# Attention with q/k norm, then a gated MLP: whole gated units before attention, rstd behind the exponential, and earlier transfer issues

## Chip, cores, metric

One core of one Trainium2 chip. The metric is device time of one execution in microseconds (us), the median of several; spans and stages come from one profiled execution per kernel. The same kernel varies by about 1% from execution to execution, so small differences are judged by ratios with a 95% interval. A run is called slow when it is over 1.5% above the fastest run of the same kernel; the others are fast, and ratios use fast runs alone.

## The reference, cut to what matters

```python
# q, k, v: (8 batches, 12 heads, 448, 64) f32
q_n, k_n = rmsnorm(q, g_q), rmsnorm(k, g_k)
attn = softmax(q_n @ k_n.T / 8)
x = (attn @ v) as (8, 448, 768)
h = relu(x @ w_in)                       # 768 x 1024, halves u and v
v_n = (v - mean) / sqrt(var + 1e-6)
gated = u * (w_spatial @ v_n + b_spatial)
out = gated @ w_out                      # 512 x 768
```

## The kernel before

Heads are taken in 24 groups of four (three groups a batch). A group has seven passes of scores; after 20 early passes (steps 0 to 9) the kernel goes in steps of two passes, 10 to 83. Each step does scores on TensorE, one exponential on ScalarE, and beside it either an attention (three weighings of 16 matmuls) or a slice of the gated MLP of an earlier batch. GpSimd squares and scales q and k and issues the v and weight transfers; VectorE reduces and empties PSUM.

```python
work = deque()                       # gated work, one matmul per entry
def fill(us_of_pe):
    debt[0] = min(debt[0] + us_of_pe, us_of_pe)
    while work and (debt[0] > 0 or work[0][0] == 0):
        cost, fn = work.popleft(); debt[0] -= cost; fn()
# a unit (v: 6 matmuls, u: 6, spatial: 4, out: 4) takes one of four PSUM
# buffers at its first matmul and is emptied after its last

def early(p):                        # ... cut
    if p == 3:
        rstd(1); scaled(1, 0, eng=dve); scaled(1, 1, eng=dve); after((1, 1))
        load_v(0, range(5)); load_w_in(1)
    elif p == 8:
        rstd(2); scaled(2, 0, eng=dve); scaled(2, 1); squares(3, 0); squares(3, 1)
    # ...
for s in range(S0, NST):             # S0 = 10, NST = 84
    scores(pss[:, 0:2], 2 * s); scores(pss[:, 2:4], 2 * s + 1)
    prep(s, True)                    # rstd of the groups due in this step
    expo(pss, 2 * s, 2)
    prep(s, False)                   # reductions, scaling, squares, transposes, loads
    # ...
    if s == 11: load_v(1, range(5))
    if s == 13: load_w_sp()
    if s == 21: load_w_out()
    # ...
    if s in busy: attend(...)        # three weighings: three PSUM buffers
    else: fill(rate)
```

`rstd` is a logarithm and an exponential on ScalarE over the reduced squares.

## Time and profile before

| | before |
|---|---|
| median | 312.6 us (310.65 to 316.51 in the first four) |
| span of the profiled run | 312.4 us |
| exponential of step 10, 14, 25, 83 starts at | 45.00, 60.43, 100.64, 281.61 us |
| TensorE idle, step 25 to 83 | 180.97 - 172.17 = 8.80 us |
| half-clock windows after the start | at 31.9, 59.2, 79.7, 96.7 us, 3.4 us each |

The start of the exponential of a step is my clock through the program. "Early" below is up to step 25, "steady" is step 25 to 83, and then come some 30.7 us of the last batch. In a wait line, "A <- B: total, times, longest" is idle time of A's engine ended by B. Line numbers in a profile are kept from the kernel before, so `L379` is weighing, `L350` scores, `L357` the exponential, `L385` the first instruction of the reciprocal of the sums (which frees the first weighing's PSUM buffer), `L330` the k scale.

This is the view of TensorE's waits in the steady stretch of the kernel before:

```profile
PE pss L350 <- ACT et L357: 2.5, 4, 1.0
PE ps L379 <- ACT rc L385: 1.7, 3, 0.6
PE pss L350 <- DVE kT L330: 1.6, 2, 0.9
PE ps L530 <- DVE osb L435: 1.4, 3, 0.5
```

Six kinds of wait (the four largest are shown; 8.5 us in all), none above 1 us at a time.

### The profile page before, as it was taken

How to read it: one execution, taken by the hardware profiler on the slowest of the kernel's cores; microseconds unless marked ns; L12 is line 12 of the kernel's file. 1: busy time of each engine (PE TensorE's matmuls, PEld its weight loads, DVE VectorE, ACT ScalarE, POOL GpSimd, SP SyncE). 2: the span in 40 equal slices, each digit the busy share in tenths (PEclk: the TensorE clock that was granted, in tenths of full speed). 3: DMA queues.
4: the chain of work that ended last, by engine and by line, in shares of the span. 5: the costliest groups of instructions: out<-in, count | busy, mean ns of one | idle time of the engine just before them, and what ended most of it. 6: DMA issues, size and time to landing. Idle time of an engine off the chain costs nothing.

```text
span 312.4 us, 6419 instructions
## 1 busy us (share of the span) xinstructions
PE 275.7 (88%) x2541; PEld 128.2 (41%) x2541; DVE 208.4 (67%) x360; ACT 205.5 (66%) x260; POOL 201.9 (65%) x185
## 2 busy tenths in 40 slices
PE   7585769599797999998999899989999999999994
PEld 7342324244243444334434443444343444444552
DVE  3863465596675674795896777768867955754652
ACT  2676487489393797758677776866877866765421
POOL 3245679939996499749983999569966960400300
PEclk9789799799797999999999999999999999999999
DMA  7899997966999979999979999999851595121135
GB/s 168 200 248 190 228 213 112 139 156 132 177 138 235 208 125 245 220 223 131 233 100 224 212 135 257 245 162 178 147 96 27 58 201 101 27 101 52 25 153 177
DMA packets 97504, 49.98 MB, mean 160 GB/s; under 512 B 67009, under 2 KB 93826, under 8 KB 97474
## 3 DMA queue, kind: packets, MB, share of 16 engines
q1 hardware_dynamic: 74562, 40.71, 61.5%
q0 software_dynamic: 21552, 8.27, 23.8%
q10 hardware_dynamic: 1360, 0.59, 0.8%
q8 instruction: 20, 0.33, 0.4%
q14 instruction: 10, 0.08, 0.1%
HBM read 38.55 MB, written 11.01 MB: 159 GB/s over the span
## 4 chain that ended last, share of the span: by engine, by line
PE 46%; POOL 14%; DVE 14%; DMA 9%; ACT 8%; issue 6%; SPq 2%; POOLq 0%; DVEq 0%
PE ps L530 9%; PE ps L379 9%; PE ps L458 9%; PE ps L498 7%; PE pss L350 6%; POOL sqt L233 6%; ACT et L357 5%; DMA qb<-in_q_dram 3%; POOL n L260 3%; POOL vn L480 3%; DMA vt<-in_v_dram 3%; DVE ms L241 3%; PE ps L488 2%; DVE s L466 2%; DMA w_out<-in_moe_w_out_dram 2%
## 5 line engine op out<-in xcount | busy, mean ns | idle before, releaser
L357 ACT ACTIVATE et<-pss 128x1792 bf16<-128x1792 f32 x74 | 122.8, 1659 | 48.0 <-PE pss L350 46.3
L241 DVE TENSOR_REDUCE ms<-sqt 128x14 f32<-128x896 f32 x46 | 49.3, 1076 | 13.9 <-POOL sqt L233 13.9
L393 DVE TENSOR_TENSOR xt<-ps,rc 128x448 bf16<-128x448 f32 x48 | 27.9, 619 | 40.9 <-ACT rc L386 40.8
L530 PE MATMUL ps<-w_out,gt 128*128 128x384 bf16 (+1 forms) x256 | 48.9, 333 | 4.1 <-DMA w_out<-in_moe_w_out_dram 2.3
L458 PE MATMUL ps<-w_in_v,xt 128*128 128x512 bf16 (+1 forms) x192 | 48.1, 389 | 0.0
L379 PE MATMUL ps<-et,vt 128*32 128x448 bf16 x768 | 43.1, 359 | 5.5 <-DMA vt<-in_v_dram 3.8
L350 PE MATMUL pss<-qT,kT 64*128 64x448 bf16 x254 | 37.6, 359 | 11.4 <-ACT et L357 5.0
L260 POOL TENSOR_TENSOR n<-kb,rs 128x896 bf16<-128x896 f32 x22 | 38.6, 1753 | 5.4 <-issue 4.5
L488 PE MATMUL ps<-xt,w_in_u 128*128 128x448 bf16 x192 | 40.6, 354 | 1.3 <-ACT vs L427 0.8
L476 POOL TENSOR_SCALAR nm<-mv 128x4 f32<-128x4 f32 x8 | 1.8, 223 | 57.9 <-DVE mv L467 50.1
L233 POOL TENSOR_TENSOR sqt<-qb 128x896 f32<-128x896 f32 x21 | 36.1, 1719 | 0.1
L233 POOL TENSOR_TENSOR sqt<-kb 128x896 f32<-128x896 f32 x21 | 35.3, 1681 | 0.6 <-DMA kb<-in_k_dram 0.6
L435 DVE COPY osb<-ps 128x384 f32<-128x384 f32 (+1 forms) x50 | 27.2, 556 | 12.0 <-PE ps L530 10.5
L260 POOL TENSOR_TENSOR n<-qb,rs 128x896 bf16<-128x896 f32 x18 | 30.5, 1694 | 5.9 <-ACT rs L250 5.7
L530 PEld LDWEIGHTS <-gt 128*128 128x128 bf16 (+1 forms) x256 | 24.7, 102 | 22.1 <-issue 8.6
L379 PEld LDWEIGHTS <-vt 128*32 128x32 bf16 x768 | 21.0, 98 | 22.9 <-DMA vt<-in_v_dram 4.5
L116 POOL DMA_DIRECT2D vt<-in_v_dram x40 | 29.3, 739 | 0.0
L498 PE MATMUL ps<-w_spT,vn 128*128 128x448 bf16 (+1 forms) x128 | 28.7, 369 | 0.3 <-DVE w_spT L209 0.3
L480 POOL TENSOR_SCALAR vn<-vs,nm,rv 128x512 bf16<-128x512 bf16 (+1 forms) x32 | 24.0, 762 | 7.5 <-ACT rv L475 5.1
L350 PEld LDWEIGHTS <-kT 64*128 64x128 bf16 x276 | 10.3, 94 | 41.2 <-issue 28.3
L458 PEld LDWEIGHTS <-xt 128*128 128x128 bf16 (+1 forms) x192 | 18.0, 102 | 21.8 <-issue 7.3
L488 PEld LDWEIGHTS <-w_in_u 128*128 128x128 bf16 x192 | 17.3, 98 | 22.5 <-issue 8.9
(84 smaller groups left out, 325.5 us busy)
## 6 DMA issues: line engine op xcount, KB each, us to landing
out_dram<-osb SPq DMA_DIRECT2D x24, 384.0 KB, 4.4
qb<-in_q_dram SPq DMA_DIRECT2D x7, 576.0 KB, 5.5
qb<-in_q_dram SPq DMA_DIRECT2D x14, 288.0 KB, 6.6
kb<-in_k_dram SPq DMA_DIRECT2D x7, 576.0 KB, 7.6
kb<-in_k_dram SPq DMA_DIRECT2D x14, 288.0 KB, 7.4
vt<-in_v_dram POOLq DMA_DIRECT2D x8, 288.0 KB, 5.4
vt<-in_v_dram POOLq DMA_DIRECT2D x16, 144.0 KB, 4.4
qb<-in_q_dram SPq DMA_DIRECT2D x22, 96.0 KB, 5.3
```

The lines of the kernel that those rows point to most:

```text
L116: pool.dma_start(out=t[r, hs, D * c:D * (c + n)], in_=x)
L233: pool.tensor_tensor(out=t, in0=x, in1=x, op=ALU.mult)
L241: dve.tensor_reduce(out=sqs[gk][:, key[1], :], in_=sqt.pop(key).rearrange("p h c d -> p (h c) d"), axis=AX.X, op=ALU.add)
L260: (eng or pool).tensor_tensor(out=t.rearrange("p c h d -> p h c d"), in0=raw[key], in1=rst[gk][:, key[1], :].rearrange("p (h c) -> p h c", ...
L350: pe.matmul(out=ps[:, h, 0:S], lhsT=kT[r, c0:c0 + 128], rhs=qT[r, :], start=True, stop=True, tile_position=(64 * h, 0))
L357: act.activation(out=ets[s][:, 2 * a:2 * a + 2 * m, :], in_=ps[:, 0:2 * m, 0:S], func=AF.Exp, bias=0.0, scale=1.0)
L379: pe.matmul(out=ps[32 * l:32 * l + 32, 0:S], lhsT=w, rhs=et_of(G, 3 if r == 3 else r + 4 * y, h), start=(r == 0), stop=(r == 3), tile_posi ...
L458: pe.matmul(out=ps[0:m, :], lhsT=xts[b][:, j, t0:t0 + m], rhs=w_in_v[:, j, :], start=(j == 0), stop=(j == 5), tile_position=(0, 0))
L480: pool.tensor_scalar(out=vn_t[b % 2][0:m, c, :], in0=vs[b][c][0:m, :], scalar1=nms[b][0:m, c:c + 1], scalar2=rvs[b][0:m, c:c + 1], op0=ALU ...
L488: pe.matmul(out=ps[:, 0:S], lhsT=w_in_u[:, j, 128 * f:128 * f + 128], rhs=xts[b][:, j, :], start=(j == 0), stop=(j == 5))
L498: pe.matmul(out=ps[:, 0:S], lhsT=vn_t[b % 2][0:kp, c, 128 * f:128 * f + 128], rhs=w_spT[0:kp, c, :], start=(c == 0), stop=(c == NT - 1))
L530: pe.matmul(out=ps[o:o + m, 0:384], lhsT=gts[b][f][:, t0:t0 + m], rhs=w_out[:, f, r], start=(f == 0), stop=(f == 3), tile_position=(0, o))
```

## The change

Intent: leave no unit half done over an attention, keep the rstd chain from holding up exponentials, and use GpSimd's idle time for transfers needed soon.

```diff
-            for part in (0, 2, 3):
+            for part in (0, 2):          # part 3 (first Y rows) now from GpSimd
                 load_part(0, i, part, g)
...
-    def fill(us_of_pe):
+    def fill(us_of_pe, whole):
         debt[0] = min(debt[0] + us_of_pe, us_of_pe)
-        while work and (debt[0] > 0 or work[0][0] == 0):
+        while work and (debt[0] > 0 or work[0][0] == 0 or (whole and not work[0][2])):
...
-            fill(rate)
+            fill(rate, s + 1 in busy)
...
     squares(0, 1, 0)
+    for g in (1, 2):
+        for i in (1, 0):
+            load_part(0, i, 3, g, pool)
...
     after((0, 1, 1))
-    squares(2, 1)
+    load_v(0, range(5))
...                                        # early(3)
-            load_v(0, range(5))
+            squares(2, 1)
...                                        # early(8)
             squares(3, 1)
+            load_v(1, range(5))
...
-            if (what == "rstd") != early_act:
+            if (what == "rstd" and G < 5) != early_act:
...
-        if s == 11:
-            load_v(1, range(5))
-        if s == 21:
+        if s == 19:
             load_w_out()
```

`part 3` is one piece of the "Y rows", the rows of q and k of batch 0's heads 6 to 11; `w_in_v` and `w_in_u` below are the two halves of `w_in`. `work[0][2]` is true at the first matmul of a unit. In the list of a batch's gated work the second u unit also moves ahead of the layer norm's rstd and application.

More of the change, by code (lines that the diff above doesn't have):

```diff
@@ L445, in one @@
                 done(cell[0])
-        return [(each, lambda i=i: one(i)) for i in range(n)]
+        return [(each, lambda i=i: one(i), i == 0) for i in range(n)]
     def tokens(c):
@@ L548, in tails, with also @@
         ot = unit_o(b - 1, 3, 0) + unit_o(b - 1, 3, 1)
-        seq = [(0.216 * i, 0.12, fn) for i, (_, fn) in enumerate(vt)]
-        seq += [(0.163 * i - 0.01, 0.08, fn) for i, (_, fn) in enumerate(ot)]
-        return [(cost, fn) for _, cost, fn in sorted(seq, key=lambda x: x[0])]
+        seq = [(0.216 * i, 0.12, u[1]) for i, u in enumerate(vt)]
+        seq += [(0.163 * i - 0.01, 0.08, u[1]) for i, u in enumerate(ot)]
+        return [(cost, fn, i == 0) for i, (_, cost, fn) in enumerate(sorted(seq, key=lambda x: x[0]))]
     work = deque()
+    def also(fn):
+        work.append((0, fn, True))
     def gated(b):
-        work.extend(unit_v(b, 0) + unit_v(b, 1) + [(0, lambda: stats(b, 0))])
-        work.extend(unit_v(b, 2) + [(0, lambda: stats(b, 1))])
-        work.extend(tails(b) + [(0, lambda: stats(b, 2)), (0, lambda: stats(b, 3))])
-        work.extend(unit_u(b, 0) + [(0, lambda: ln_rstd(b))])
-        work.extend([(0, lambda c=c: ln_apply(b, c)) for c in range(NT)])
-        for f in (1, 2, 3):
-            work.extend(unit_u(b, f))
+        work.extend(unit_v(b, 0) + unit_v(b, 1))
+        also(lambda: stats(b, 0))
+        work.extend(unit_v(b, 2))
+        also(lambda: stats(b, 1))
+        work.extend(tails(b))
+        also(lambda: stats(b, 2))
+        also(lambda: stats(b, 3))
+        work.extend(unit_u(b, 0) + unit_u(b, 1))
+        also(lambda: ln_rstd(b))
+        for c in range(NT):
+            also(lambda c=c: ln_apply(b, c))
+        work.extend(unit_u(b, 2) + unit_u(b, 3))
         if b == 0:
-            work.append((0, bias_row))
-            work.extend((0.5, lambda sc=sc: w_sp_unit(sc)) for sc in range(NT))
+            also(bias_row)
+            work.extend((0.5, lambda sc=sc: w_sp_unit(sc), True) for sc in range(NT))
         else:
@@ L572 @@
     debt = [0.0]
-    def fill(us_of_pe):
+    def fill(us_of_pe, whole):
         debt[0] = min(debt[0] + us_of_pe, us_of_pe)
-        while work and (debt[0] > 0 or work[0][0] == 0):
-            cost, fn = work.popleft()
+        while work and (debt[0] > 0 or work[0][0] == 0 or (whole and not work[0][2])):
+            cost, fn, _ = work.popleft()
             debt[0] -= cost
```

## The prediction

> **What bounds the kernel now.** I read the page's slices first, then the waits of TensorE, then the timelines. From the page, busy tenths of TensorE and its granted clock in 40 slices of 7.8 us:
> ```profile
> PE   7585769599797999998999899989999999999994
> ...
> PEclk9789799799797999999999999999999999999999
> ```
> From slice 13 (about 100 us) TensorE is full and its clock whole; before that there are holes, and each low clock digit sits at or just after one. The busy time of the engines in stretches (busy us with counts for PE, PEld, DVE, ACT, POOL; clock, DMA share, GB/s) puts sizes on it:
> ```profile
> 20.00:40.00 20.00, 13.01 (x148) 6.36 (x150) 10.09 (x13) 12.13 (x19) 10.96 (x13) 0.91 1.28 214
> 40.00:60.00 20.00, 14.18 (x157) 6.17 (x153) 11.82 (x16) 13.04 (x19) 18.58 (x18) 0.98 1.07 157
> ...
> 80.00:100.00 20.00, 16.37 (x116) 6.85 (x115) 11.91 (x21) 10.47 (x13) 19.11 (x15) 0.84 1.17 183
> ```
> TensorE idles about 5.8 us a 20 us stretch up to 60 us, and 3.6 us in 80 to 100. In 100 to 280 the same view sums to 171.2 us busy of 180: only 8.8 us are idle there. After 282 us comes the last batch, nearly all TensorE. So the gain must come mostly from the first 100 us.
>
> The waits of the whole run (us in total, times, longest) name the holes:
> ```profile
> ACT et L357 <- PE ps L379: 7.1, 1, 7.1
> ...
> POOL w_in_v L189 <- DMA vt<-in_v_dram: 3.8, 1, 3.8
> PE ps L379 <- DMA vt<-in_v_dram: 3.8, 2, 2.2
> ...
> PE pss L350 <- ACT rs L250: 3.1, 1, 3.1
> ...
> PE ps L530 <- DMA w_out<-in_moe_w_out_dram: 2.3, 1, 2.3
> ```
> **Hole A** (28.8 to 35.9 us): v of batch 0, issued at 21.52, lands at up to 32.2; the first weighted sum waits, and the exponential after it waits for a probability buffer that this sum still reads. **Hole B** (56 to 59.5) is in these timeline rows (start, duration; last, the idle time before and what ended it):
> ```profile
> 52.45 3.53 POOL L116 DMA_DIRECT2D vt<-in_v_dram  x5
> 55.95 1.74 POOL L233 TENSOR_TENSOR sqt<-kb 128x896 f32<-128x896 f32 x1
> 57.72 1.09 DVE L241 TENSOR_REDUCE ms<-sqt 128x14 f32<-128x896 f32 x1 [3.57 <-POOL sqt L233]
> 58.84 0.32 ACT L249 ACTIVATE ln<-ms,eps 128x28 f32<-128x28 f32 x1 [3.37 <-DVE ms L241]
> 60.43 1.66 ACT L357 ACTIVATE et<-pss 128x1792 bf16<-128x1792 f32 x1 [1.01 <-PE pss L350]
> ```
> Five v issues hold GpSimd, so a square, its reduction and the rstd behind it are late; rstd stands ahead of other exponentials in ScalarE's queue, and everything stops. **Hole C** is w_out, 2.3 us at 94 to 97. In the steady part the waits of TensorE from 164 to 229 us, two batches, are small:
> ```profile
> PE pss L350 <- ACT et L357: 1.0, 1, 1.0
> PE pss L350 <- DVE kT L330: 0.9, 1, 0.9
> PE ps L379 <- ACT rc L385: 0.6, 1, 0.6
> PE ps L530 <- DVE osb L435: 0.4, 1, 0.4
> ```
>
> **What the Trainium skill says.** "TensorE: Matmul & The Clock Gate", Part 1: the array falls to half clock after an idle window of some 3.4 us. The trace agrees: half-clock stretches of 3.4 us follow A, B and C (from 31.9, 59.2 and 96.7 us), so removing a hole also removes up to 1.7 us of slowness. The same page, Architectural detail: ScalarE, VectorE and GpSimd are strict FIFO; hole B is such a queue. "DMA: Bandwidth & Descriptors", Issuing engines are not separate DMA queues: moving an issue to another engine saves the sequencer's time only. The trace agrees that there is no spare transfer time early: the DMA share is 1.28 in 20 to 40 us and queue traffic is gapless up to 47 us. The same page, Latency and other measured facts: a first byte takes longer from GpSimd (about 1 us against 0.6). Here the two tiny GpSimd loads at 1.45 us landed after 3.9 us, the hardware queues' 96 KB early ones after 3.4 to 4.7.
>
> **The change, part by part.**
> 1. *v of batch 0 early.* GpSimd issues it after its 14.88 us copy instead of at 21.5: about 6.5 us sooner, ahead of the squares of group 2 k. With the loaded latency of 8.1 to 8.8 us it lands by 15.1+3.6+8.5 = 27.2, against a need at 28.2. Without it exponential 12 could start near 31 (scores at 28.9, weighing 0.94, transposes 0.56, scores 0.36, half of the second weighing 0.5) instead of 35.9: gross 4.9 us. Given back: v, 688 KB as stored at some 170 KB/us, takes 4 us of a saturated transfer system before batch 1's k, which landed near 29 us; w_in_v then shares as well, so k lands at 32.5 to 35.5. Its square (1.68) and reduction (1.09) lead to rstd of group 3 at 36 to 39 instead of 39.9. GpSimd also has v of batch 1 (3.53 us) to issue before scaling group 3, which TensorE already awaited for 0.4 us at 43.2. I take **-2.5 us** net of the 4.9.
> 2. *First Y rows by GpSimd.* Four issues of 0.6 us leave the sync queue and take 4 x 0.7 = 2.8 us in GpSimd's 3.15 us gap after 7.75 us. They cannot be issued earlier, so group 1's rows land near 12.0 to 12.8, while its squares ran at 11.09 (GpSimd) and 11.74 (ScalarE). I expect the start to slip by about 0.9 us, hidden later by the transfers; it is in the 2.5.
> 3. *v of batch 1 early.* 3.53 us leave GpSimd's busy stretch at 52 (18.58 of 20 us) for its 4.49 us gap at 36 to 40.6. With *rstd behind the exponential* (from group 5 on) hole B goes: 3.1 us plus part of a half-clock window, 1.0. Against it I set 0.6, because GpSimd stays full: **-3.5 us**.
> 4. *w_out two steps earlier.* Steps 19 and 21 are some 6 us apart; hole C needs 2.3. It vanishes, with most of its cold window, 0.7 us: **-3.0 us**.
> 5. *Whole units and rstd order, steady part.* Per two batches: the 1.0 (an exponential behind an rstd that waited for VectorE), the 0.6 (a half-done unit holds one of four PSUM buffers over attention), and some of the 0.9 and 0.4. Over 2.8 such periods about 2.3 x 2.8 = 6.4 us can go. Against it: I replayed the list of units with its debt rule. Steps before attention grow by up to 1.1 us (a v unit of 6 x 0.217), and the step after attention shrinks to 1.4 to 2.3 us of TensorE work, below the 2.35 us that scores, exponential (1.66) and handing over need; some ten such steps lose 0.1 to 1.0 us each, 3 us together. rstd 1.7 us later delays the scaling and the transposes, which have about a step of slack. Net **-3.0 us**.
> 6. *First u and second u before the layer norm:* order alone; its statistics are ready sooner, GpSimd's waits for them (4.3 and 3.9 us) are not TensorE's. 0. The last 30 us: 0.
>
> Sum: 2.5 + 3.5 + 3.0 + 3.0 = 12.0; 311.45 - 12.0 = **299.5 us**.
>
> **Rivals.** *Transfers take all of part 1:* gapless traffic to 47 us speaks for it; against it, what rstd 3 needs is less than all that had landed by 35.5 us. Time: 302. *The hole simply closes:* holes A, B and C at their full size with cold windows, 6 + 4.4 + 3.5, and steady 5: 292.5; GpSimd being 19.11 of 20 us busy in 80 to 100 speaks against it, since its chain (scale, square, v issue, scale, square, from 73.3 to 82.5) already sets a k scale and a 1.3 us wait at 83.4. *GpSimd becomes the bound up to 100 us:* then parts 3 and 4 give 3 instead of 6.5: 303. *Short steps starve TensorE:* part 5 turns to +2: 304.5. All may meet in part, giving about 307.
>
> **Range and chances.** The four terms can each be wrong by some 2 to 3 us and lean on shared causes, so 80% is 293.5 to 305.5. The 2% line is 305.2, just inside the upper end: faster 0.88, within 2% 0.11, slower 0.01, since no work is added to TensorE.
>
> **What would show it.** (1) right if the 7.1 us wait of ScalarE is under 3 and the first v lands before 28; wrong if batch 1's k lands at 33 or later and its square waits longer than 3 us. (2) squares of group 1 start after 11.7. (3) no wait of 3 us for rstd near 55. (4) no wait for w_out. (5) TensorE's idle time over the 180 us before the last batch falls from 8.8 to about 6, the waits on the recip's logarithm are gone, and short idles appear before exponentials in the step after attention. If the saving lies elsewhere than in the first 100 us, my weighting was wrong.

## The result

The changed kernel took 301.14 us (298.94 to 302.04, 4 runs) against 312.58 beside it: ratio 0.9643, 95% interval 0.9554 to 0.9733. A ratio is the mean time of one kernel's fast runs over that of the other's fast runs of the same rounds, so it is not quite the ratio of the medians. On chip 3, six runs of the same kernel gave 302.11 and 0.9623 (0.9557 to 0.9689). Predicted were 299.5 (293.5 to 305.5) and faster.

The profiled pair differs by more (312.4 and 296.9 us of span) than the medians, because the profiled run of before was a longish one (314.23) and that of after the shortest of four. Stages must be read with that in mind, and I use a second profile of the changed kernel (called control) beside the first.

The page's slices after: busy tenths of TensorE and its granted clock.

```profile
PE   8387769988599999999999999999999999999994
...
PEclk9879999999989999999999999999999999999998
```

The low clock digits at slices 4 and 7 are gone; one remains near 80 us (a half-clock window from 80.3), and the row of nines begins at slice 11 (82 us) instead of 13 (102 us). The busy time by stretches (length; PE, PEld, DVE, ACT, POOL busy; clock, DMA share, GB/s), the stretches of the view of before and the one that it left out:

```profile
20.00:40.00 20.00, 14.90 (x193) 7.30 (x192) 12.60 (x15) 15.40 (x24) 14.18 (x15) 1.00 1.28 223
40.00:60.00 20.00, 15.61 (x173) 6.80 (x171) 15.75 (x24) 14.26 (x18) 14.62 (x14) 1.00 0.98 155
60.00:80.00 20.00, 15.27 (x136) 7.39 (x136) 14.04 (x23) 14.05 (x18) 18.25 (x16) 1.00 0.88 166
80.00:100.00 20.00, 19.48 (x179) 8.10 (x180) 15.52 (x29) 14.46 (x17) 16.30 (x13) 0.91 1.09 171
```

TensorE gets 45 more matmuls into the first stretch (35 in the control, the second profile) at a whole clock, while the DMA share stays 1.28: the transfers are as full as before. The stretch from 60 to 80 us has less work in it than before (15.27 us busy against 18.68; the same time, though not the same steps). More than half of its idle time is one wait, which ends at 80.10 and is the longest that is left after 40 us: the scores wait for a k scale, which stands in VectorE's queue behind a reduction, which waited for a square of GpSimd (a line of VectorE's timeline and one of TensorE's):

```profile
77.90 1.09 DVE L241 TENSOR_REDUCE ms<-sqt 128x14 f32<-128x896 f32 x1 [2.40 <-POOL sqt L233]
80.10 0.81 PE L350 MATMUL pss<-qT,kT 64*128 64x448 bf16 x4 [2.68 <-DVE kT L330]
```

It is 2.67 us in the control and was 1.30 us before, and the half-clock window left near 80 us follows it. So part of what the closed holes gave was lost again here. The waits of TensorE in the steady stretch after:

```profile
PE ps L488 <- DVE vs L429: 0.9, 2, 0.5
PE pss L350 <- DVE kT L330: 0.7, 2, 0.4
PE ps L530 <- DVE xt L393: 0.2, 1, 0.2
PE pss L350 <- ACT et L357: 0.2, 1, 0.2
```

That is all of them, 2.0 us where six kinds had 8.5 (3.2 in the control, 1.2 of it one wait for an emptied output). By stages:

| stage | before | after | control |
|---|---|---|---|
| exponential of step 10 | 45.00 | 42.81 | 44.24 |
| exponential of step 14 | 60.43 | 55.74 | 58.84 |
| exponential of step 25 | 100.64 | 93.75 | 96.34 |
| steady stretch, step 25 to 83 | 180.97 | 172.46 | 173.55 |
| rest | 30.8 | 30.7 | 30.7 |
| TensorE idle in the steady stretch | 8.80 | 2.36 | 3.44 |

So the early part gave 4.3 to 6.9 us, for which I had predicted 9.0, and the steady part 7.4 to 8.5, for which I had predicted 3.0. The total came out near by luck: the two errors cancelled. The experiments ask which part of the change did which.

### The profile page after: what moved, and what is told of

It is laid out like the page before. It is cut to its first block, busy times and chain, and to the rows that moved or that the text cites.

```text
span 296.9 us, 6418 instructions
## 1 busy us (share of the span) xinstructions
PE 269.2 (91%) x2541; PEld 126.3 (43%) x2541; DVE 211.8 (71%) x363; ACT 203.6 (69%) x257; POOL 203.9 (69%) x189
## 3 DMA queue, kind: packets, MB, share of 16 engines
q0 software_dynamic: 21744, 8.66, 24.9%
## 4 chain that ended last, share of the span: by engine, by line
PE 39%; POOL 16%; DMA 13%; DVE 9%; SPq 8%; issue 7%; ACT 6%; POOLq 0%; DVEq 0%; ACTq 0%
SPq L107 8%; DMA kb<-in_k_dram 7%; PE ps L458 7%; PE ps L379 7%; POOL sqt L233 7%; PE ps L488 7%; PE ps L530 7%; PE pss L350 5%; PE ps L498 4%; POOL n L260 4%; ACT et L357 4%; POOL vt L116 3%; DMA kr<-n 3%; DVE ms L241 3%; DVE kT L330 2%
## 5 line engine op out<-in xcount | busy, mean ns | idle before, releaser
L530 PE MATMUL ps<-w_out,gt 128*128 128x384 bf16 (+1 forms) x256 | 47.1, 327 | 0.7 <-DVE gt L502 0.3
L458 PE MATMUL ps<-w_in_v,xt 128*128 128x512 bf16 (+1 forms) x192 | 45.9, 381 | 0.0
L350 PE MATMUL pss<-qT,kT 64*128 64x448 bf16 x254 | 37.7, 357 | 6.4 <-DVE kT L330 3.8
L379 PE MATMUL ps<-et,vt 128*32 128x448 bf16 x768 | 42.1, 357 | 1.2 <-DMA vt<-in_v_dram 1.2
L488 PE MATMUL ps<-xt,w_in_u 128*128 128x448 bf16 x192 | 39.9, 353 | 0.9 <-DVE vs L429 0.9
L233 POOL TENSOR_TENSOR sqt<-kb 128x896 f32<-128x896 f32 x21 | 35.3, 1682 | 4.1 <-DMA kb<-in_k_dram 4.0
L530 PEld LDWEIGHTS <-gt 128*128 128x128 bf16 (+1 forms) x256 | 24.1, 101 | 20.6 <-issue 7.9
L435 DVE COPY osb<-ps 128x384 f32<-128x384 f32 (+1 forms) x46 | 25.1, 555 | 10.2 <-PE ps L530 9.2
L498 PE MATMUL ps<-w_spT,vn 128*128 128x448 bf16 (+1 forms) x128 | 27.2, 353 | 0.4 <-DVE w_spT L209 0.4
L466 DVE BATCH_NORM_STATS2 s<-vs 128x6 f32<-128x512 bf16 (+1 forms) x32 | 21.7, 678 | 1.5 <-ACT vs L427 1.2
```

Of the source, the lines that this page charges most:

```text
L233: pool.tensor_tensor(out=t, in0=x, in1=x, op=ALU.mult)
L350: pe.matmul(out=ps[:, h, 0:S], lhsT=kT[r, c0:c0 + 128], rhs=qT[r, :], start=True, stop=True, tile_position=(64 * h, 0))
L379: pe.matmul(out=ps[32 * l:32 * l + 32, 0:S], lhsT=w, rhs=et_of(G, 3 if r == 3 else r + 4 * y, h), start=(r == 0), stop=(r == 3), tile_posi ...
L458: pe.matmul(out=ps[0:m, :], lhsT=xts[b][:, j, t0:t0 + m], rhs=w_in_v[:, j, :], start=(j == 0), stop=(j == 5), tile_position=(0, 0))
L488: pe.matmul(out=ps[:, 0:S], lhsT=w_in_u[:, j, 128 * f:128 * f + 128], rhs=xts[b][:, j, :], start=(j == 0), stop=(j == 5))
L498: pe.matmul(out=ps[:, 0:S], lhsT=vn_t[b % 2][0:kp, c, 128 * f:128 * f + 128], rhs=w_spT[0:kp, c, :], start=(c == 0), stop=(c == NT - 1))
```

## The experiments

Twelve runs, all correct (the first four rows on chip 12, the others on chip 3). Each undoes one thing of the changed kernel unless it says otherwise. The table has the ratio to before of the fast runs, then stages of the profiled run in us.

| run | what | median | ratio (95%) | step 10 | step 14 | step 25 | steady |
|---|---|---|---|---|---|---|---|
| u_whole | units not finished before attention | 308.21 | 0.9839 (0.9766, 0.9912) | 42.71 | 54.55 | 94.32 | 179.76 |
| u_rstd | rstd ahead of the exponential | 299.66 | 0.9557 (0.9497, 0.9617) | 44.18 | 58.38 | 95.02 | 172.27 |
| u_steady | both, and the order of the u units | 306.61 | 0.9778 (0.9673, 0.9882) | 42.38 | 54.24 | 91.80 | 181.11 |
| u_order | order of the u units | 302.54 | 0.9660 (0.9604, 0.9716) | 44.36 | 58.56 | 96.09 | 174.08 |
| u_v0 | v of batch 0 late | 303.77 | 0.9719 (0.9666, 0.9772) | 46.13 | 59.06 | 96.53 | 173.65 |
| u_v1 | v of batch 1 late | 304.64 | 0.9738 (0.9672, 0.9805) | 43.01 | 58.07 | 98.39 | 173.04 |
| u_yrows | Y rows on the sync queue | 304.45 | 0.9743 (0.9693, 0.9793) | 46.93 | 62.16 | 98.01 | 172.59 |
| u_wout | w_out at step 21 | 306.25 | one fast run | 42.93 | 55.85 | 93.86 | 172.46 |
| u_wout2 | the same again (profile of a slow run) | 302.58 | 0.9635 (0.9578, 0.9693) | 43.56 | 57.76 | 98.86 | 173.07 |
| r_after | control: the changed kernel | 302.11 | 0.9623 (0.9557, 0.9689) | 44.24 | 58.84 | 96.34 | 173.55 |
| i_winv | w_in_v issued later | 306.46 | 0.9734 (0.9665, 0.9803) | 47.61 | 61.71 | 99.25 | 173.64 |
| i_best | that, and three more moves | 299.53 | 0.9600 (0.9541, 0.9659) | 41.56 | 56.87 | 93.00 | 173.82 |

The columns differ in how far to trust them. The steady stretch falls into two groups with nothing between: 172.27 to 174.08 for every kernel with whole units, 179.76 to 181.11 for every one without. Step 10 and 14 of one and the same kernel differ by 1.4 and 3.1 us between two profiles (after and control), so one look there shows only larger things. A half-clock window in the early part, which comes in some executions and not in others, is part of that spread: the control had one of 6.8 us from 43.4 us, the first profile none between 19 and 80. By ratio, u_whole and u_yrows lie clear of the control's interval; u_steady, u_v0, u_v1 and i_winv overlap its upper end (0.9689) by 0.0024 at most, so for these the ratio and the stage have to agree.

### Whole units

```diff
-            fill(rate, s + 1 in busy)
+            fill(rate, False)
```

> The changed kernel with units no longer finished before an attention step; all else kept. The stretch from the exponential of step 25 to that of step 83 took 180.97 us before and 172.46 after. Theory (the PSUM buffer held over attention, and its late eviction, was most of the steady loss): the stretch goes back up by 4 to 6 us, waits of TensorE on the recip's logarithm come back (1.7 us, 3 times), time about 306 (ratio to before 0.98). Rival (rstd ahead of the exponential was most of it): up by less than 2 us, time about 302.5.

The steady stretch went back to 179.76 us, up 6.2 to 7.3, and the ratio to 0.9839, which is 0.0196 to 0.0216 above the changed kernel's two, or 6.1 to 6.8 us of 312.6. The waits of TensorE in the steady stretch of this run:

```profile
PE pss L350 <- DVE kT L330: 2.8, 4, 0.9
PE ps L379 <- ACT rc L385: 1.7, 3, 0.6
...
```

The waits on the reciprocal are back exactly, three times 0.6, as the theory had it. TensorE's timeline of this run shows how the rest hangs on the same thing:

```profile
159.68 0.94 PE L379 MATMUL ps<-et,vt 128*32 128x448 bf16 x16 [0.56 <-ACT rc L385]
...
161.16 0.40 PE L458 MATMUL ps<-w_in_v,xt 128*64 128x512 bf16 x1
161.16 0.35 PE L530 MATMUL ps<-w_out,gt 128*64 128x384 bf16 x1
...
167.10 0.55 PE L350 MATMUL pss<-qT,kT 64*128 64x448 bf16 x4 [0.87 <-DVE kT L330]
```

Two units were left with one matmul to go before this attention. They hold two of the four PSUM buffers, so the third weighing (159.68) waits until the reciprocal has read the first. Their last matmuls run only at 161.16, behind the attention. Their emptying and statistics then stand in VectorE's queue behind the attention's stores, with a k scale behind them, and the scores at 167.10 wait for it. With whole units this emptying is done during the attention, when VectorE otherwise waits for the reciprocal: its stores of attention output waited 40.8 us in all on the reciprocal before, 27.0 after (28.1 in the control, 39.1 in this run). VectorE's waits for the reciprocal were the free time that the change filled.

### rstd behind the exponential

```diff
-            if (what == "rstd" and G < 5) != early_act:
+            if (what == "rstd") != early_act:
```

> The changed kernel with rstd ahead of the exponential for every group, as before. Theory (whole units matter more): the stretch from step 25 to 83 grows by 2 to 3 us (four waits of the scores on a late exponential, 2.5 us before), and the exponential of step 14 hardly moves (no v issue stands before the reduction of group 5 now, which ends at 53.0 with the exponential at 55.7): time about 303.5. Rival (rstd order carries the steady gain): stretch up by 5 us or more, time 306 or more. Third view: hole B comes back by 2 us or more at step 14.

Both my theory (2 to 3 us) and the rival (5 or more) failed: the stretch was 172.27 us, equal to the changed kernel's, and the ratio 0.9557 was no worse than 0.9643 and 0.9623. The waits of this run's steady stretch:

```profile
PE pss L350 <- ACT et L357: 2.2, 4, 1.3
PE pss L350 <- DVE kT L330: 0.3, 1, 0.3
```

The four late exponentials are there, 2.2 us, but the total idle time of TensorE was 172.27 - 169.34 = 2.93 us, against 2.36 and 3.44 in the two profiles of the changed kernel. Removing this wait brought others of nearly its size. What the new place of rstd costs is seen on GpSimd: it waited 23.8 us (control 26.5) for rstd before scaling, against 10.1 in this run and 6.5 before. One of these waits, 4.9 to 6.5 us before the scaled k of group 5, is early; it is 2.0 in this run. Whether the old order is truly a little better is left open, as the intervals overlap.

### The transfers alone

```diff
-            fill(rate, s + 1 in busy)
+            fill(rate, False)
-            if (what == "rstd" and G < 5) != early_act:
+            if (what == "rstd") != early_act:
-        work.extend(unit_u(b, 0) + unit_u(b, 1))
+        work.extend(unit_u(b, 0))
...                                        # the second u unit behind ln_apply
```

> The changed kernel with whole units, the place of rstd and the order of the u units all put back: only the transfer moves (v of batches 0 and 1, Y rows, w_out) stay. If the parts add up, the stretch from step 25 to 83 is 181 us again and the exponential of step 25 still comes 5 to 7 us earlier than before (100.64 in its profile): time about 307 (ratio 0.982). Rival (the early gain is lost again where the steady part is bound by its own chain, so the transfer moves are worth little alone): time within 2 us of before.

The first view was right: the steady stretch is 181.11 us, that of before to 0.2 us, while step 25 came at 91.80 instead of 100.64. By the ratio the transfers are worth 0.0222, or 6.9 us. With rstd ahead of the exponential, as before, step 14 still came at 54.24. So hole B of the prediction is not a matter of rstd's place. What fits is that GpSimd no longer issued v of batch 1 there; four transfers moved at once here, and u_v1 below undoes this one alone. In a strict queue, which the prediction took as given, rstd ahead of an exponential blocks only when what it waits for is late. Here the lateness was the cause, and moving rstd only treats the effect.

### Order of the u units

```diff
-        work.extend(unit_u(b, 0) + unit_u(b, 1))
+        work.extend(unit_u(b, 0))
...                                        # the second u unit behind ln_apply
```

> The changed kernel with the second u unit again behind the layer norm's rstd and its application, all else kept. Theory (order alone, worth nothing): stretch from step 25 to 83 within 0.7 us of 172.46, time within 1 us of the changed kernel. Rival (the later layer norm is what keeps ScalarE from waiting on the statistics: 7.9 us of such waits before, 3.2 after): stretch up by 2 to 3 us, time about 303.5.

The stretch was 174.08, 1.6 us above the first profile of the changed kernel but 0.5 above the control, and the median 302.54 beside the control's 302.11. The rival's 2 to 3 us did not come. Within this spread the order is worth nothing.

### v of batch 0, v of batch 1

```diff
 u_v0:                                     u_v1:
     after((0, 1, 1))                          squares(3, 1)
-    load_v(0, range(5))                   -   load_v(1, range(5))
+    squares(2, 1)                         ...
...                                        +   if s == 11:
-            squares(2, 1)                 +       load_v(1, range(5))
+            load_v(0, range(5))
```

> The changed kernel with v of batch 0 issued at its old place, after the squares and scaling of group 1, all else kept. Theory (v of batch 0 is the first hole; its early landing moves exponential 12 by 2.5 us and the first full step by 2.2): exponential 12 goes back from 33.4 to about 36.5 us, the exponential of step 10 from 42.8 to about 45; time about 303.5. Rival (the transfers are saturated and work-conserving up to 47 us, so the order among them is worth nothing at step 10): exponential of step 10 within 0.8 us of 42.8.

The theory held. Exponential 12 started at 37.04 us (33.40 and 33.27 in the two profiles of the changed kernel, 32.5 to 35.3 in all twelve with v of batch 0 early) and step 10 at 46.13 (42.81, 44.24). The ratio is 0.0076 to 0.0096 higher: 2.4 to 3.0 us. In the changed kernel the wait is smaller but not gone. ScalarE's timeline of the changed kernel:

```profile
33.40 4.16 ACT L357 ACTIVATE et<-pse 128x896 bf16<-128x896 f32 x5 [3.31 <-PE ps L379]
```

I had put this exponential at about 31. v was issued at 15.7, near the 15.1 predicted, but took 9.2 to 13.0 us to land instead of the 8.5 that I carried over, so the weighing still waited 1.0 us on its last part.

> The changed kernel with v of batch 1 issued at step 11 again, rstd of group 5 staying behind the exponential. Theory (the five issues, 3.53 us of GpSimd, were hole B): step 10 comes up to 1 us earlier (GpSimd scales group 3 without them), steps 10 to 14 take 3 us longer than the 11.8 to 12.9 us without a cold window, or the wait appears one step later in the scaled rows of group 5; step 21 about 3 us later. Time about 304. Rival (rstd behind the exponential alone closes hole B): step 14 and 21 within 1 us.

The theory held here too, one step later. Step 10 was no later than in the changed kernel; from step 14 to 21 it took 28.9 us instead of 25.2 (25.0 in the control), with a wait of TensorE of 3.6 us for the scaled rows of group 5 and a half-clock window of 6.8 us from 63.3. The ratio is 0.0095 to 0.0115 higher: 3.0 to 3.6 us. That GpSimd's 3.53 us of issues were the cause is thereby shown with rstd in its new place; u_steady, where four transfers moved together, agrees with it for the old one.

### The Y rows

```diff
-            for part in (0, 2):
+            for part in (0, 2, 3):
...
-    for g in (1, 2):
-        for i in (1, 0):
-            load_part(0, i, 3, g, pool)
```

> The changed kernel with the four transfers of Y rows back on the sync queue. Theory (they land later from GpSimd and hold up group 1's squares): first exponential at 13.0 to 13.2 instead of 14.0, exponential 12 and step 10 at most 1 us earlier since transfers and GpSimd set those; time within 1.5 us, rather lower. Rival (the sync queue's issue time bounded the early loads, so undoing this costs): step 10 later by over 1 us.

Here my theory fell and the rival held. The first exponential did come at 13.06 instead of 14.02 us (13.33 in the control; 13.3 to 15.3 in all profiles with the Y rows from GpSimd), so the Y rows do land later from GpSimd. But step 10 came at 46.93, 2.7 to 4.1 us later, and the ratio was 0.0100 to 0.0120 higher: 3.1 to 3.8 us. A half-clock window of 10.2 us, from 44.1, goes with it. GpSimd's timeline of this run shows where:

```profile
37.71 1.68 POOL L233 TENSOR_TENSOR sqt<-kb 128x896 f32<-128x896 f32 x1 [8.72 <-DMA kb<-in_k_dram]
39.33 3.53 POOL L116 DMA_DIRECT2D vt<-in_v_dram  x5
```

and the same in the changed kernel:

```profile
34.13 1.68 POOL L233 TENSOR_TENSOR sqt<-kb 128x896 f32<-128x896 f32 x1 [3.19 <-DMA kb<-in_k_dram]
35.75 3.54 POOL L116 DMA_DIRECT2D vt<-in_v_dram  x5
```

The square of batch 1's k waits for its transfer, the v issues stand behind the square, and the scaling of group 3 behind those (it started at 42.83 us in this run, at 39.25 in the changed kernel). This k is last in the sync queue of this phase. With four issues less before it the sync queue finished issuing it at 22.6 us instead of 24.7. With the Y rows on the sync queue its square started at 37.71; in the eight other fast profiles with v of batch 0 and the Y rows early and w_in_v in its place (the changed kernel, its control, u_wout, u_whole, u_rstd, u_order, u_steady and u_v1) it started between 33.2 and 35.4.

That the move pays is shown against the control; by which of two ways is not. Without the four issues GpSimd is free sooner too: w_in_v left it at 21.9 us instead of 23.9 (22.8 in the control), and i_winv below shows that the place of w_in_v alone moves this k. Of the 2.4 to 3.7 us by which the last piece of k landed later here (37.6), 1.2 to 1.8 are its later issue and the rest is a longer time under way (landings worked out from the traces). No run separates the two.

### w_out

```diff
-        if s == 19:
+        if s == 21:
             load_w_out()
```

> The changed kernel with w_out issued at step 21 again. Theory: its landing, 7.4 us after an issue at about 85 us, comes at about 92 against a need at 91.7, in the middle of the combined tail; so the stretch from step 21 to 25 grows by 1 to 3 us over 12.8 and a half-clock window may follow; time about 303. Rival (nothing: the issue lands in time because step 21 itself is now late for its own reason, a k scale): no wait for w_out, time within 1 us.

> w_out at step 21 again, a second time, now beside the control: its first profile equalled the changed kernel's up to 0.1 us with a wait of 0.5 us for w_out, but three of its four times were 305 to 308. Theory (the landing is only just in time, and in most executions late enough for a wait of 2 us and a half-clock window): median 3 to 5 us above the control. Rival (that chip or chance): within 1.5 us of the control.

The control ran beside the second try:

> The changed kernel itself, unaltered, as control on the chip of this call: 301 us (298.9 to 302.0 earlier), ratio to before 0.964; stretch from step 25 to 83 of 172.5 us.

The first profile equals the changed kernel's to 0.12 us in every stage of the table, with a wait of 0.5 us for w_out; the other three times, 305.37 to 307.96, count as slow and are not used. Beside the control, the fast runs give 0.9635 against 0.9623: no difference. The profiled run of the second try is itself slow; it has a wait of 4.2 us for w_out and 16.1 us from step 21 to 25 (12.5 in the control). As only a slow run shows it, I do not build on it. The wait of 2.3 us in the kernel before was real, and w_out at step 19 removes it safely, but a gain in fast runs is not shown. On one core slow is only a rule about time, so leaving slow runs out could also leave out executions in which w_out came late. Whether a late w_out makes an execution slow, or the other way round, stays open.

### Later issues of w_in_v, and a version with three more moves

```diff
 i_winv:
             squares(2, 1)
-            load_w_in(1)
...
             squares(3, 1)
+            load_w_in(1)
             load_v(1, range(5))
```

> The changed kernel with w_in_v issued after the squares of group 3 instead of before the scaling of group 2. Theory (what sets step 10 is the landing of batch 1's k, 34.0 us in the changed kernel, behind v of batch 0 and w_in_v): k lands by 32, its square starts by 32.2 instead of 34.1; but the issues of w_in_v and v then hold GpSimd till about 39, so the scaling of group 3 and step 10 (42.8) move by less than 1 us; time within 1 us of the control. Rival (the order of GpSimd's transfers does not touch the sync queue's): k lands at 34 as before.

The mechanism was right: the square of k started at 31.56 instead of 34.13 and 35.38, so transfers from GpSimd do hold up those of the sync queue. The consequence was wrong, and the run is slower than the control (ratio 0.9734 against 0.9623). GpSimd's timeline:

```profile
33.18 2.32 POOL L189 DMA_DIRECT2D w_in_v<-in_moe_w_in_dram  x4
35.46 2.86 POOL L116 DMA_DIRECT2D vt<-in_v_dram  x4
42.88 0.66 POOL L116 DMA_DIRECT2D vt<-in_v_dram  x1 [4.55 <-DMA w_in_v<-in_moe_w_in_dram]
```

The ninth issue in a row waits 4.55 us until the first of the eight before it has landed, and the scaling of group 3 waits behind it, to 43.55 us. The prediction's line "POOL w_in_v <- DMA vt", 3.8 us before, was the same thing: five v issues, three of w_in_v, and the fourth waits.

```diff
 i_best, besides:
-            load_v(1, range(5))            # not after the squares of group 3
+            load_v(1, range(5))            # after those of group 4
-            load_w_in(0)                   # at pass 16
+            if s == 12: load_w_in(0)
-            if (what == "rstd" and G < 5) != early_act:
+            if (what == "rstd" and G < 6) != early_act:
```

> As the last, and besides: v of batch 1 issued after the squares of group 4, the first half of w_in at step 12 in GpSimd's idle time, and rstd of group 5 ahead of its exponential again (others behind). Theory: GpSimd scales group 3 at rstd's end, near 37.8, so step 10 comes at 41.5 to 42.0 instead of 42.8; the 1.95 us stall of TensorE at 60.6 goes; step 25 about 2 to 3 us earlier; time 1 to 3 us under the control. Rival (GpSimd and VectorE before step 21 set it anyway): step 21 within 0.7 us of 80.9 and no gain.

Step 10 came at 41.56 and the wait for rstd before the scaled k of group 5 fell from 6.5 us in the control to 0.2, as expected; the stall of TensorE for the scaled q of group 5 did not go (1.1 us). At 299.53 and a ratio of 0.9600 it is 2.6 us below the control by medians, but the intervals overlap almost wholly. The rival's mark was met in part: step 21 came at 81.09, within 0.7 us of the changed kernel's 80.94 (83.86 in the control), with the 2.67 us wait for the k scale still before it. It beats the kernel before clearly, the changed kernel not demonstrably.

## Why the prediction was right, and where it was not

- **What bounds the kernel:** right in kind, wrong in proportion. The holes up to 100 us were the larger ones to look at, but about half of the gain came from 8.8 us of idle time that I had called small. A reading was off as well: TensorE idled 7.0 us, not 5.8, in 20 to 40 us (20 - 13.01).
- **Part 1, v of batch 0, -2.5:** the size was right: undoing it costs 2.4 to 3.0 us, and step 10 moved by 2.2 us in the first profile (0.8 in the control). By its own marks it was not. ScalarE's wait fell to 3.3 us (4.3 in the control), not under 3. The first part of v landed at 24.9, but the last at 31.5 instead of 27.2. And the sign named for being wrong came: k of batch 1 landed at 33.9 (35.1 in the control) and its square waited 3.2 us. That landing lies in the 32.5 to 35.5 us that the part itself had given back for, so the sign contradicted the estimate; the saving stood.
- **Part 2, Y rows, hidden:** the slip of the start agrees in the profiled pair (0.9 predicted, 0.99 measured), but was 0.30 in the control; "hidden" was right, but the step left out the other side. Moving the issues brings batch 1's k forward, worth 3.1 to 3.8 us. I had read from "DMA: Bandwidth & Descriptors", Issuing engines are not separate DMA queues, that only sequencer time is saved, and took that for little. Here the queue that lost the issues ended in the transfer for which GpSimd's square waited; whether its own shorter issue or the later w_in_v brought this k forward is not separated.
- **Part 3, v of batch 1 and rstd, -3.5:** the sum right (3.0 to 3.6 by undoing the v issue alone), the cause half wrong: no contribution of rstd's place shows there.
- **Part 4, w_out, -3.0:** not shown. The wait is gone, but undoing the move costs the fast runs nothing measurable.
- **The early sum, -9.0:** the transfers alone give 8.8 us at step 25 in the profile and 6.9 by the ratio. In the changed kernel it is 4.3 to 6.9; the spread of one look is too wide to say more than that the early terms overlap instead of adding, since 2.7 + 3.3 + 3.4 by undoing each is already more than what they give together. The new wait of 2.7 us for the k scale before step 21, with its half-clock window, is in both profiles of the changed kernel and had no term in the sum.
- **Part 5, -3.0 (from 6.4 less 3, which is 3.4):** the failed term. Its gross gain, 6.4 us, was about right: idle time fell by 5.4 to 6.4 us. The loss set against it, 3 us from short steps behind attention, was not there: scores waited 0.2 us for an exponential in the whole stretch, once. The steps behind attention, put at 1.4 to 2.3 us of TensorE work, took 2.31 to 3.22 from exponential to exponential; step 50, the one with that wait, took 2.41. One reason is in its timeline: nine output matmuls took 1.64 us (0.18 each), where the program's own list, which the replay used, has 0.163. A further 2.1 us came from TensorE's busy time (172.17 to 170.10), which I had not foreseen. I also gave rstd a share that whole units alone have: without them the stretch is 180 us, without rstd's move it is 172.
- **Rivals:** "transfers take all of part 1" failed, though transfers do set step 10. "GpSimd becomes the bound" fits the two terms that it named: it gave parts 3 and 4 together 3 us, and undoing them costs 3.0 to 3.6 and nothing measurable; the k scale that it named, 1.3 us before, waits 2.7 us now. "The hole simply closes" (292.5) did not come. "Short steps starve TensorE" failed.

## What to carry to other kernels

In a loop bound by one engine, do not leave a unit half done across a phase that needs the same rotating buffers: its cost is not only the buffer, but that its emptying arrives late in another engine's strict queue and delays what stands behind it. Sum such waits over the whole run before calling them small, and count where the waiting engine's neighbours have free time. When a queue stalls on a late input, look for what made the input late before moving the instruction that waits. In a phase with saturated transfers, find the transfer on which the next stage waits, and clear the way before that one: here that helped even though the four transfers moved for it landed later. After closing a hole, read the same stretch again for the wait that takes its place.

## What the Trainium skill lacked or had wrong

- "DMA: Bandwidth & Descriptors", Issuing engines are not separate DMA queues, says that several issuing engines save only sequencer time, usually small. Here four issues less on one saturated queue, with w_in_v leaving GpSimd 0.9 to 1.9 us later, moved the square that waits for the queue's last transfer from 37.7 to between 33.2 and 35.4 us, and the time by 3.1 to 3.8 us.
- The same page, Latency and other measured facts, has about 1 us for the first byte from GpSimd. With the sync queue full, the first v transfers were issued at 21.5 us in the kernel before and the packets of that queue start at 25.5 us in its trace; from issue to landing v of batch 0 took 8.1 to 8.8 us there and 9.2 to 13.0 in the changed kernel, against 2.9 to 7.4 for the later batches in the kernel before.
- No page that I read has it: of transfers issued from GpSimd, the ninth waits until the first of the eight before it has landed (3.8 us before, 4.6 in i_winv, 4.4 in u_v0, 0.4 in the control). Whether that is the queue's limit or comes from how the program hands out its semaphores, no run shows.
- "TensorE: Matmul & The Clock Gate", Part 1, has the clock fall after an idle window of about 3.4 us, and the prediction said that the trace agrees. It agrees in the 3.4 us length of the half-clock windows there (other runs have 6.8 and 10.2 us), not in the idle time before them: in the 3.4 us before the four windows of the kernel before TensorE was busy for 0.37, 0.54, 2.41 and 1.17 us, its longest gap there was 3.1 us, and the window at 79.7 followed none of the holes (longest gap 0.5 us). It also varies between executions: of two profiles of the same changed kernel one has a half-clock stretch at 43.4 us, of 6.8 us, and the other none between 19 and 80.
